# Attention's outputs normalized after the product with the values and transposed back

## The chip, the cores and the metric

The kernel runs on one core of a Trainium2 chip. Its time is the device time of one execution in microseconds. A matmul runs on TensorE (PE in the rows; PEld is its weight load), elementwise work on VectorE (DVE), ScalarE (ACT) and GpSimd (POOL); DMAs are issued mostly from SyncE's queue (SP). TensorE and the others exchange data through eight PSUM banks of 512 f32 columns on 128 partitions; GpSimd reaches SBUF only.

## The reference

Four batches, eight heads, 512 local and 32 global tokens, head size 64. A local query sees the 32 global keys and the local keys within 32 positions; a global query sees all 544. Two feed-forward nets follow. Cut to what matters:

```python
def sm(s):                                   # softmax over the last axis
    s = s - np.max(s, axis=-1, keepdims=True)
    e = np.exp(s)
    return e / (np.sum(e, axis=-1, keepdims=True) + 1e-09)
k_all, v_all = np.concatenate([k_g, k_l], axis=2), np.concatenate([v_g, v_l], axis=2)
out_g = np.matmul(sm(scale * np.matmul(q_g, k_all.transpose(0, 1, 3, 2))), v_all)
s_ll = np.where(np.abs(pos[:, None] - pos[None, :]) <= 32, scale * (q_l @ k_l^T), -1e9)
s_l = np.concatenate([scale * (q_l @ k_g^T), s_ll], axis=-1)
out_l = np.matmul(sm(s_l), np.concatenate([v_g, v_l], axis=2))
x = concatenate([out_g, out_l], axis=2), heads side by side   # 2176 tokens x 512
h = x @ moe_w_in;   x = (h * np.cos(h)) @ moe_w_out            # 512 -> 2048 -> 512
h = np.maximum(x @ moe2_w_in, 0.0);   out = (h * h) @ moe2_w_out
```

The factors on the inputs make the scores wide, so that the maximum in `sm` matters.

## The kernel before

*Attention.* The work is cut into 16 pairs p of heads (batch p // 4) and 8 global units g (two pairs each). Queries of a pair are cut into 8 tiles of 64, each against its window of 128 local keys and the 32 global ones. For a pair, TensorE transposes keys and queries (`tr_k`, `tr_q`, tiles tk, tq); `s_mm` makes 16 score blocks (s). VectorE's `top` scales, masks and finds the row maximum (line 372), eight per pair; ScalarE's `exp` (line 385) makes exponentials and row sums. `recip` (lines 396, 400) turns the sums into factors, and `norm` (line 415 on VectorE, 420 on GpSimd) and `norm_g` (line 404) multiply the probabilities pt by them. TensorE transposes the result (`tr_w`, `tr_g`, tiles tw and tg), and `g_mm` and `v_mm` multiply by the values: the values are the stationary operand, the probabilities stream, and the outputs o come with the 128 head coordinates on the rows, as the nets want them in xt. `o_evac` copies them there. The global unit does the same with 64 queries of two pairs at once (`s_mm`, `exp`, `norm` at line 530, `tr_w`, `tr_l`, `o_mm` at line 557, which writes og).

*PSUM.* Banks 0 and 1 take transposes in turn, bank 2 a score block and tg, banks 3 to 5 scores, banks 6 and 7 the outputs.

*The nets.* Weights come as 64-bit numbers: `conv` loads a raw tile of 512 KB (lines 92, 97) into one of two buffers, and ScalarE, VectorE and GpSimd make f32 from it (lines 115 to 138). `w_in` and `w_out` sum and split weights, `x_prep` sums and splits inputs (lines 147, 160, 653, 665). A step of a net has seven products (ha, he, hb by bank, line 785) and output products y (line 877); 48 steps run one after the other. The high half of a step's result g can be written only once the attention's last tiles are closed.

*Order.* Every operation is an `Op` with durations by engine. `att_graph` calls the pieces of the attention in a written sequence, and that sequence is TensorE's. The other queues are filled by a planner: it walks time forward, gives each engine the ready operation with the least due time (`latest`), and lets operations that two engines can do go to either. Each engine then runs its queue strictly in that order. `beside`, `d_v2` and `d_g2` price the operations that VectorE and GpSimd share.

## Time and profile before

| | us |
|---|---|
| three runs: median (lowest, highest) | 874.5 (872.16, 874.72) |
| profiled execution, its time | 873.02 |
| its span, first to last instruction | 871.2 |
| TensorE busy | 845.6 |
| VectorE busy | 666.0 |
| GpSimd busy | 558.2 |
| ScalarE busy | 533.7 |

The span is what the trace covers; the time has 1.82 us around it. The attention fills the first 147 us of the span, and the first output product of the nets starts at 164 us. Busy time is an average over stages of different kinds, so the rows further down are taken by stretch.

### The profile page before, as it was taken

Reading aid. Unit: us, or ns where it says so; the run is one execution under the profiler, and the core shown is the slowest. Engines: PE = TensorE matmul, PEld = TensorE weight load, DVE = VectorE, ACT = ScalarE, POOL = GpSimd, SP = SyncE. Lnnn points to the kernel's source line nnn. Section 1 sums busy time; section 2 is a strip of 40 time slices with the busy share of each in tenths; the row PEclk is TensorE's granted clock in tenths of the full one; section 3 lists DMA queues with packets and bytes.
Section 4 is the critical chain, followed back from the end, with each engine's and each line's share of the span. In section 5 each row is a group of like instructions: output and inputs, shape, how many; then the busy total and the mean of one; then the engine's idle time right before and its main releaser. Section 6 shows DMA issues by size and latency. Waiting matters only on the chain.

```text
span 871.2 us, 17208 instructions
## 1 busy us (share of the span) xinstructions
PE 845.6 (97%) x6028; PEld 781.6 (90%) x6028; DVE 666.0 (76%) x1541; ACT 533.7 (61%) x1279; POOL 558.2 (64%) x614
## 2 busy tenths in 40 slices
PE   8979997999999999999999999999999999999997
PEld 7758775899998999999999998889898989898886
DVE  6868989999799687868787799988766767454544
ACT  5867996878776566656665777756544554343331
POOL 4446799899877574557556799988444747332221
PEclk9998998899999999999999999999999999999999
DMA  9889864347865666675667366586774687346733
GB/s 174 184 219 202 188 180 170 134 183 255 313 240 202 221 218 236 224 236 183 233 238 258 135 217 250 185 271 237 271 233 143 241 297 225 131 163 247 215 120 83
DMA packets 134038, 182.00 MB, mean 209 GB/s; under 512 B 60736, under 2 KB 114496, under 8 KB 133952
## 3 DMA queue, kind: packets, MB, share of 16 engines
q1 hardware_dynamic: 130256, 179.73, 62.9%
q10 hardware_dynamic: 3696, 1.18, 0.6%
q8 instruction: 48, 0.79, 0.4%
q14 instruction: 38, 0.31, 0.1%
HBM read 141.03 MB, written 35.65 MB: 203 GB/s over the span
## 4 chain that ended last, share of the span: by engine, by line
PE 87%; ACT 4%; DVE 4%; POOL 2%; DMA 1%; issue 1%; SPq 0%; ACTq 0%; POOLq 0%
PE y L877 42%; PE hb L785 16%; PE he L785 11%; PE ha L785 10%; ACT pt L385 2%; PE tw L425 2%; PE s L360 1%; PE o L463 1%; PE tq L311 1%; PE tk L302 1%; PE sg L491 1%; PE spin L620 1%; POOL wf L138 1%; DMA raw<-in_moe_w_in_dram 1%; PE o L448 1%
## 5 line engine op out<-in xcount | busy, mean ns | idle before, releaser
L147 POOL TENSOR_TENSOR g<-cr,g 128x384 fp32r<-128x384 f32 (+1 forms) x192 | 202.2, 1060 | 161.9 <-ACT g L836 157.1
L888 DVE TENSOR_TENSOR xt<-y,xt 128x384 f32<-128x384 f32 (+2 forms) x287 | 170.2, 595 | 88.9 <-PE y L877 87.9
L877 PE MATMUL y<-g,wo 128*128 128x384 f32 (+1 forms) x1152 | 217.1, 326 | 0.0
L877 PE MATMUL y<-wo,g 128*128 128x512 f32 x816 | 209.5, 393 | 0.0
L877 PEld LDWEIGHTS y<-g,wo 128*128 128x128 f32 x1152 | 193.8, 188 | 0.0
L877 PEld LDWEIGHTS y<-wo,g 128*128 128x128 f32 x816 | 150.0, 188 | 24.3 <-DVE wo L147 0.2
L785 PE MATMUL hb<-xs,wi 128*128 128x384 f32 (+1 forms) x864 | 167.0, 328 | 4.4 <-ACT s L793 4.0
L785 PEld LDWEIGHTS hb<-xs,wi 128*128 128x128 f32 x864 | 147.9, 189 | 10.5 <-ACT s L793 4.5
L785 PE MATMUL he<-xs,wi 128*128 128x384 f32 (+1 forms) x576 | 111.9, 329 | 2.9 <-DVE cr L828 2.9
L785 PE MATMUL ha<-xs,wi 128*128 128x384 f32 (+1 forms) x576 | 111.7, 329 | 0.3 <-ACT ptg L513 0.3
L836 ACT ACTIVATE g<-cr 128x384 fp32r<-128x384 f32 (+1 forms) x192 | 95.5, 503 | 24.3 <-DVE cr L828 23.6
L785 PEld LDWEIGHTS he<-xs,wi 128*128 128x128 f32 x576 | 98.8, 189 | 8.1 <-DVE cr L828 4.0
L138 POOL TENSOR_TENSOR wf<-wf,cc 128x512 uint32<-128x512 uint32 x64 | 86.8, 1357 | 24.5 <-DVE wf L126 18.0
L785 PEld LDWEIGHTS ha<-xs,wi 128*128 128x128 f32 x576 | 98.3, 189 | 2.5 <-ACT ptg L513 0.5
L131 DVE SCALAR_TENSOR_TENSOR cc<-raw,cc 128x512 uint32<-128x512 uint32 x64 | 67.3, 1056 | 0.0
L822 ACT ACTIVATE cr<-cr,halfpi 128x384 f32<-128x384 f32 (+1 forms) x96 | 56.3, 592 | 8.2 <-DVE cr L817 7.3
L793 ACT ACTIVATE s<-hb 128x384 f32<-128x384 f32 (+1 forms) x48 | 22.7, 473 | 54.1 <-PE hb L785 53.1
L385 ACT ACTIVATE pt<-pt,st 128x160 f32<-128x160 f32 x128 | 53.1, 419 | 3.4 <-DVE st L372 3.4
L147 POOL TENSOR_TENSOR wi<-ws,wi 128x512 fp32r<-128x512 f32 x25 | 34.3, 1375 | 27.7 <-ACT wi L171 18.0
L126 DVE TENSOR_SCALAR wf<-wf 128x512 uint32<-128x512 uint32 x64 | 47.0, 737 | 6.5 <-ACT wf L115 4.0
L793 ACT ACTIVATE s<-he 128x384 f32<-128x384 f32 (+1 forms) x48 | 22.6, 471 | 42.9 <-PE he L785 42.8
L122 ACT ACTIVATE cc<-raw 128x512 uint32<-128x512 uint32 x64 | 42.3, 668 | 7.9 <-DMA raw<-in_moe_w_in_dram 7.2
(141 smaller groups left out, 1298.1 us busy)
## 6 DMA issues: line engine op xcount, KB each, us to landing
xs<-xs_T SPq DMA_DIRECT2D x48, 768.0 KB, 5.8
xs<-xs_B SPq DMA_DIRECT2D x36, 768.0 KB, 5.4
raw<-in_moe_w_in_dram SPq DMA_DIRECT2D x32, 512.0 KB, 5.5
raw<-in_moe_w_out_dram SPq DMA_DIRECT2D x32, 512.0 KB, 4.6
xs<-xs_T SPq DMA_DIRECT2D x24, 640.0 KB, 5.5
xs_T<-xs SPq DMA_DIRECT2D x16, 768.0 KB, 3.6
xs<-xs_B SPq DMA_DIRECT2D x18, 640.0 KB, 5.5
xs_B<-xs SPq DMA_DIRECT2D x12, 768.0 KB, 4.4
```

The lines of the kernel that those rows point to most:

```text
L122: A.activation(v, raw[q, m, c][:, :, 0].bitcast(U32), AF.Copy, scale=2.0**-29)
L126: V.tensor_scalar(u, u, 3, None, op0=ALU.logical_shift_left)
L131: V.scalar_tensor_tensor(v, t[:, :, 1].bitcast(U32), 0x80000000, v, op0=ALU.bitwise_and, op1=ALU.bitwise_or,)
L138: G.tensor_tensor(u, u, v, op=ALU.add)
L147: eng.tensor_tensor(lo, x, hi.bitcast(F32), op=ALU.subtract)
L385: nc.scalar.activation(self.pt[hb][:, u, :], self.pt[hb][:, u, :], AF.Exp, bias=self.st[hb][:, 0, u : u + 1], scale=-1.0, accum_out=self.s ...
L785: nc.tensor.matmul(out, lhsT=w[:, ws, c : c + P], rhs=xs[:, xh, kk, 0:n], start=start and k == 0, stop=k == 5, skip_group_check=True,)
L793: A.activation(self.sb[name], self.hold(bank_name), AF.Copy)
L822: A.activation(self.r[key], self.r[key], AF.Sin, bias=halfpi, scale=TWOPI)
L836: A.activation(GT[s, f][0][:, th * n : th * n + n], self.r[key], AF.Copy)
L877: nc.tensor.matmul(o, lhsT=l, rhs=r, start=k == 0, stop=k == 5)
L888: V.tensor_tensor(dst, y, dst, op=ALU.add)
```

## The change

The probabilities stay unnormalized. `tr_w` transposes the exponentials as they are, and GpSimd's `gather` copies the global columns without a factor. In `g_mm` and `v_mm` the operands change places: the transposed probabilities are stationary and the values stream, so that o has 64 queries of two tiles on the rows and the head coordinates on the columns. A query's factor is then one number per row, and `o_norm` (VectorE, two per pair) multiplies by it while it moves o from PSUM to the new tile OS. `tr_o` transposes OS back, four transposes per pair (tile to), and one `o_evac` per pair copies 128x512 into xt. `recip` works once per pair on eight sums. The global unit's `o_mm` writes [query, head coordinate] with 32-wide stationary tiles; `places` puts its factor into the column of the head's half, `o_norm` and one transpose (tog) bring it back.

PSUM banks 0, 1, 2 and 5 take transposes in turn (`TBANK`); scores lie in 3, 4, 6 and 7, beside the outputs in 6 and 7. The sequence of the attention is now a string, `ORDER`. In the planner, operations on SBUF that use the port shared by VectorE and GpSimd carry `port` and follow one another on it; their durations are lower; what is planned early is due 30 earlier and raw loads 60, where both had 20, and the lag of the first loads is 4.0 where it was 2.5; `BIAS` changes from 6 to -100.

```diff
-    ST = [lp.tile([P, 4, 4], F32, name=f"st{i}") for i in range(4)]
+    ST = [lp.tile([P, 4, 8], F32, name=f"st{i}") for i in range(4)]
...
+    OS = lp.tile([P, 2, 256], F32, name="os")
+    OG = lp.tile([P, P], F32, name="og_s")
+    odd = lp.tile([P, 2], F32, name="odd")
...
-        UNIT[hb, i, 0] = ((3, 5)[hb], i)
-        UNIT[hb, i, 1] = (4, k) if k < 3 else (2, 0)
+        for h in range(2):
+            UNIT[divmod(k, 2) + (h,)] = (3 + h, KTB * k) if k < 3 else (6 + h, 256)
+    ROUNDS = ((1, 1), (0, 0), (0, 1), (1, 0))
...
-        def recip(self, hb):
-            st = self.st[hb]
+        def recip(self):
+            st = self.st
             nc.vector.tensor_scalar(
                 st[:, 2, :], st[:, 1, :], 1e-9, None, op0=ALU.add, op1=ALU.add,
                 accum_out=st[:, 3, 0:1],
             )
             nc.vector.reciprocal(st[:, 2, :], st[:, 2, :])
-        def norm_g(self, hb):
-            nc.gpsimd.tensor_tensor(
+        def gather(self, hb):
...
+            nc.gpsimd.tensor_scalar(
                 self.pgs[:, hb].rearrange("p (i h q) -> p h i q", i=2, h=2),
                 self.pt[hb][:, :, P:KTB].rearrange("p (h i) q -> p h i q", h=2),
-                self.st[hb][:, 2, :].rearrange("p (h i) -> p h i", h=2)
-                .unsqueeze(3).to_broadcast([P, 2, 2, SG]),
-                op=ALU.mult,
+                **ONE,
...
-        def norm(self, hb, u, eng):
-            w, r = self.pt[hb][:, u, 0:P], self.st[hb][:, 2, u : u + 1]
-            if eng == "V":
-                nc.vector.tensor_scalar(
-                    w, w, r, None, op0=ALU.mult, op1=ALU.add,
-                    accum_out=self.st[hb][:, 3, u : u + 1],
-                )
-            else:
-                nc.gpsimd.tensor_scalar(w, w, r, 1.0, op0=ALU.mult, op1=ALU.mult)
...
-                    for h in range(2):
-                        d = slice(64 * h, 64 * h + 64)
+                    for half in range(2):
+                        q = slice(64 * half, 64 * half + 64)
                         nc.tensor.matmul(
-                            self.o[i][d, hb, :],
-                            lhsT=VGZ[self.b % 2][k, self.kk, d],
-                            rhs=self.tgs[k, hb, :],
+                            self.o[i][q, hb, :],
+                            lhsT=self.tgs[k, hb, q],
+                            rhs=VGZ[self.b % 2][k, self.kk, :],
...
-                for half in range(2):
-                    v = (VB if half else VA)[self.p // 2 % 2]
-                    q = slice(64 * half, 64 * half + 64)
-                    for h in range(2):
+                for h in range(2):
+                    for half in range(2):
+                        v = (VB if half else VA)[self.p // 2 % 2]
+                        q = slice(64 * half, 64 * half + 64)
                         nc.tensor.matmul(
-                            self.o[i][64 * h : 64 * h + 64, hb, q],
-                            lhsT=v[:, 2 * hb + i, 2 * (self.p % 2) + h, :],
-                            rhs=self.tws[hb][:, 2 * h + i, q],
+                            self.o[i][q, hb, 64 * h : 64 * h + 64],
+                            lhsT=self.tws[hb][:, 2 * h + i, q],
+                            rhs=v[:, 2 * hb + i, 2 * (self.p % 2) + h, :],
...
-        def o_evac(self, i, eng):
-            c0 = self.b * SL
-            dst = xt[:, self.kk, c0 : c0 + SL].rearrange("p (k i q) -> p k i q", k=2, i=2)
-            copy(eng, dst[:, :, i, :], self.o[i])
+        def o_norm(self, i):
+            nc.vector.tensor_tensor(
+                OS[:, i, :].rearrange("p (u d) -> p u d", d=D),
+                self.o[i].rearrange("p k (h d) -> p (k h) d", h=2),
+                self.st[:, 2, i::2].unsqueeze(2).to_broadcast([P, 4, D]),
+                op=ALU.mult,
+            )
+        def tr_o(self, k):
+            self.to = bank(k, "to")
+            for hb in range(2):
+                for i in range(2):
+                    c = (2 * hb + i) * P
+                    nc.tensor.transpose(
+                        self.to[:, c : c + P], OS[:, i, hb * P : hb * P + P], ident
+                    )
+        def o_evac(self, eng):
+            copy(eng, xt[:, self.kk, self.b * SL : self.b * SL + SL], self.to)
...
-        def norm(self):
-            nc.gpsimd.tensor_scalar(
-                self.pt, self.pt, self.st[:, 6:7], 1.0, op0=ALU.mult, op1=ALU.mult
+        def places(self):
+            st = self.st
+            nc.vector.tensor_scalar(
+                st[:, 8:10], odd, st[:, 6:7], None, op0=ALU.mult, op1=ALU.add,
+                accum_out=st[:, 10:11],
...
+            self.o = bank(6, "og")[:, 0:D]
             va = VA[self.gi % 2]
-            for i in range(2):
-                for c in range(5):
-                    for h in range(2):
-                        r = 128 if c < 4 else 32
-                        qs = slice((2 * i + h) * SG, (2 * i + h + 1) * SG)
-                        nc.tensor.matmul(
-                            self.o[64 * h : 64 * h + 64, i, :],
-                            lhsT=va[0:r, c, 2 * i + h, :],
-                            rhs=self.tws[:, c, qs] if c < 4 else self.tls[:, qs],
-                            start=(c == 0),
-                            stop=(c == 4),
-                            skip_group_check=True,
-                        )
-        def o_evac(self, eng):
-            c0 = NLOC + self.b * SG
-            copy(eng, xt[:, 2 * self.g : 2 * self.g + 2, c0 : c0 + SG], self.o)
+            for c in range(5):
+                r = 128 if c < 4 else 32
+                for j in range(4):
+                    qs = slice(j * SG, (j + 1) * SG)
+                    nc.tensor.matmul(
+                        self.o[qs, :],
+                        lhsT=self.tws[:, c, qs] if c < 4 else self.tls[:, qs],
+                        rhs=va[0:r, c, j, :],
+                        start=(c == 0),
+                        stop=(c == 4),
+                        skip_group_check=True,
+                    )
+        def o_norm(self):
+            nc.vector.tensor_tensor(
+                OG.rearrange("p (h d) -> p h d", h=2),
+                self.o.unsqueeze(1).to_broadcast([P, 2, D]),
+                self.st[:, 8:10].unsqueeze(2).to_broadcast([P, 2, D]),
+                op=ALU.mult,
+            )
+        def tr_o(self, k):
+            self.to = bank(k, "tog")[:, 0:P]
+            nc.tensor.transpose(self.to, OG, ident)
+        def o_evac(self, h, eng):
+            c0, d = NLOC + self.b * SG, slice(64 * h, 64 * h + 64)
+            src = self.to.rearrange("p (i h q) -> p i h q", i=2, h=2)
+            copy(eng, xt[d, 2 * self.g : 2 * self.g + 2, c0 : c0 + SG], src[d, :, h, :])
...
-    d_v2 = lambda n: 0.2 + n * 0.002
-    d_g2 = lambda n: 0.1 + n * 0.0026
+    d_v2 = lambda n: 0.14 + n * 0.00108
+    d_g2 = lambda n: 0.1 + n * 0.00235
...
-        u = Op({"G": 0.8, "A": 0.67}, lambda e: conv_u(q, m, c, e), ld, *wfree)
+        u = Op({"G": 0.66, "A": 0.67}, lambda e: conv_u(q, m, c, e), ld, *wfree)
         s = opA(0.67, lambda: conv_s(q, m, c), ld, *cfree)
-        v = opV(0.76 if beside[0] else 0.4, lambda: conv_v(q, m, c), u)
-        o = opV(1.0 if beside[0] else 0.65, lambda: conv_o(q, m, c), s, u)
+        v = opV(0.42, lambda: conv_v(q, m, c), u)
+        o = opV(0.69, lambda: conv_o(q, m, c), s, u)
+        v.port = o.port = "GV"
         raw_ring.free[j] = [o]
-        end = opG(1.4, lambda: conv_c(q, m, c), v, o)
+        end = opG(1.25, lambda: conv_c(q, m, c), v, o)
...
-    tring = Ring(2)
-    s_bank, o_bank = {k: [] for k in (2, 3, 4, 5)}, {0: [], 1: []}
-    tw_pt, pg_ring, tws_ring, tgs_ring = Ring(4), Ring(2), Ring(3), Ring(2)
+    tring, TBANK = Ring(4), (0, 1, 2, 5)
+    s_bank = {k: [] for k in (3, 4, 6, 7)}
+    tw_pt, pg_ring, tws_ring, tgs_ring, st_ring = Ring(4), Ring(2), Ring(3), Ring(2), Ring(4)
+    os_free, og_free = [], []
...
+            done = soft(lambda: None, s)
+            done.lag = 0.27 * (ROUNDS.index((hb, i)) + 1)
+            o = opE({"V": 0.245}, lambda e, a=(hb, i, h): x.top(*a), done, *slots[hb][1], *st_free)
...
+        x.norms = [opE({"V": 0.41}, lambda e, i=i: x.o_norm(i), o, x.rc, *os_free) for i in range(2)]
...
+    def back(p):
+        x = pairs[p]
+        k, needs = tbank(*x.norms)
+        o = opP("T", 0.436, lambda: x.tr_o(TBANK[k]), *needs)
+        os_free[:] = [o]
+        e = opE(on(512, "AV"), lambda e: x.o_evac(e), o)
+        tring.free[k] = [e]
+        oe[x.b, x.kk] = e
...
+    ORDER = (
+        "S:0 k:1 q:1 K:2 Qg:0 S:1 k:2 q:2 a:0 b:0 g:0 X:0 G:0 V:0 a:1 b:1 g:1 k:3 K:3 q:3 o:0 S:2 "
+        "G:1 V:1 w:0 k:4 o:1 S:3 O:0 L:2 a:2 b:2 g:2 q:4 x:0 X:1 G:2 V:2 a:3 b:3 Kg:1 g:3 k:5 K:4 "
+        "q:5 o:2 S:4 G:3 V:3 Z:2 w:1 k:6 o:3 S:5 O:1 L:3 a:4 Qg:1 b:4 g:4 q:6 x:1 X:2 G:4 V:4 a:5 "
...
-        o.latest -= 20
+        o.latest -= 30
+        if "Q" in o.on and hasattr(o, "raw"):
+            o.latest -= 30
...
+        if e in o.port:
+            o.end = port[0] = max(t, port[0]) + o.on[e]
...
-    BIAS, LOOK, drift = 6.0, 1.0, [0.0]
+    port = [0.0]
+    BIAS, LOOK, drift = -100, 1.0, [0.0]
```

**Where instructions move.** First place, TensorE's queue in the loop of the pairs, between the transposes of a global unit's probabilities (tlg, twg) and the next ones of a pair (tw, tg); s are scores, tk and tq transposes of keys and queries. Before:

```order
L541 MATMUL tlg<-ident,ptg 32x128
L537 MATMUL twg<-ident,ptg 128x128 x4
L360 MATMUL s<-kT_100,qT_107 64x160 x16
L557 MATMUL og<-tws_121,va_93 64x32 x8
L557 MATMUL og<-tls,va_93 64x32 x2
L557 MATMUL og<-tws_121,va_93 64x32 x8
L557 MATMUL og<-tls,va_93 64x32 x2
L425 MATMUL tw<-ident,pt_109 128x128 x4
L425 MATMUL tw<-ident,pt_110 128x128 x4
L430 MATMUL tg<-ident,pg_117 128x128 x2
```

Now:

```order
L553 MATMUL tlg<-ident,ptg 32x128
L549 MATMUL twg<-ident,ptg 128x128 x4
L307 MATMUL tk<-ident,kn 128x128 x4
L479 MATMUL to<-ident,os 128x128 x4
L365 MATMUL s<-kT_100,qT_107 64x160 x16
L569 MATMUL og<-va_93,tws_121 32x64 x16
L569 MATMUL og<-va_93,tls 32x64 x4
L418 MATMUL tw<-ident,pt_109 128x128 x4
L418 MATMUL tw<-ident,pt_110 128x128 x4
L423 MATMUL tg<-ident,pg_117 128x128 x2
L316 MATMUL tq<-ident,qn 128x128 x4
L588 MATMUL tog<-ident,og_s 128x128
```

Transposes of keys (tk) and of outputs (to) have come ahead of the scores, the global products og are one group of 20 instead of two of ten, and the transposes of queries and of the global outputs (tog) follow tg.

VectorE's queue at the same place, at the last top of a pair (the ISA rows: pt from scores s and a mask, and its minimum into st). Before:

```order
L280 COPY tws_120<-tw 128x512
L372 ISA pt_112,st_116<-s,mask_92 128x160
L372 ISA st_116 128x1
L280 COPY kT_101<-tk 128x7x64
L280 COPY kT_101<-tk 128x2x32
L396 TENSOR_SCALAR st_115<-st_115 128x4
L400 RECIPROCAL st_115<-st_115 128x4
```

Now, with the normalized outputs os made from o and the factors in st:

```order
L377 ISA pt_110,st_113<-s,mask_90 128x160
L377 ISA st_113 128x1
L467 TENSOR_TENSOR os<-o,st_116 128x256 x2
L126 TENSOR_SCALAR wf_1113<-wf_1113 128x512
L283 COPY kT_100<-tk 128x7x64
L283 COPY kT_100<-tk 128x2x32
```

The two os of the pair before stand behind the last top of the pair scored after it, where a recip of its own stood.

Second place, SyncE's queue, DMAs of keys and queries (kn, qn), values (va, vb, vgz) and raw weights. Before, around the first raw loads:

```order
L237 DMA va_94<-in_v_g_dram 32x4x64
L240 DMA va_94<-in_v_l_dram 96x4x64
L240 DMA va_94<-in_v_l_dram 128x4x64 x3
L240 DMA va_94<-in_v_l_dram 32x4x64
L92 DMA raw<-in_moe_w_in_dram 128x4x256 x2
L676 DMA xs_0_B_1070<-xs 128x1536
L247 DMA vb_96<-va_94 64x1024
L248 DMA vb_96<-va_94 64x1024
L230 DMA kn<-in_k_l_dram 128x4x64 x4
L230 DMA qn<-in_q_l_dram 128x4x64 x4
```

Now:

```order
L233 DMA kn<-in_k_l_dram 128x4x64 x4
L92 DMA raw<-in_moe_w_in_dram 128x4x256 x2
L240 DMA va_93<-in_v_g_dram 32x4x64
L243 DMA va_93<-in_v_l_dram 96x4x64
L243 DMA va_93<-in_v_l_dram 128x4x64 x3
L243 DMA va_93<-in_v_l_dram 32x4x64
L233 DMA qn<-in_q_l_dram 128x4x64 x4
L264 DMA qgn<-in_q_g_dram 32x8x64 x3
L259 DMA vgz_98<-in_v_g_dram 32x4x64 x4
L250 DMA vb_95<-va_93 64x1024
L251 DMA vb_95<-va_93 64x1024
L97 DMA raw<-in_moe_w_out_dram 128x1024 x2
```

The first raw loads have moved ahead of the values that follow the keys; two of w_out, which came much later, stand a few rows on.

Third place, GpSimd's queue at the end of the attention, from the last copies into pg on (xs, xr: inputs of the nets; wi, ws, wo: weights; g: results of a step). Before:

```order
L404 TENSOR_TENSOR pg_118<-pt_112,st_116 128x2x2x32
L420 TENSOR_SCALAR pt_112<-pt_112,st_116 128x128 x2
L530 TENSOR_SCALAR ptg<-ptg,stg_126 128x544
L147 TENSOR_TENSOR xs<-xr,xs 128x384 x2
L138 TENSOR_TENSOR wf_2029<-wf_2029,cc 128x512
L653 TENSOR_TENSOR xr<-xt,xr 128x384
L160 TENSOR_TENSOR ws<-wf_2029 128x256
L147 TENSOR_TENSOR wi<-wf_2029,wi 128x512
L147 TENSOR_TENSOR xs<-xr,xs 128x384
L147 TENSOR_TENSOR wi<-wf_2029,wi 128x256
L653 TENSOR_TENSOR xr<-xt 128x384 x3
L653 TENSOR_TENSOR xr<-xt,xr 128x384 x2
L147 TENSOR_TENSOR g_2756<-cr,g_2755 128x384
```

Now:

```order
L409 TENSOR_SCALAR pg_118<-pt_112 128x2x2x32
L681 TENSOR_TENSOR xr<-xt,xr 128x384
L117 TENSOR_SCALAR wf_2562<-raw 128x512
L681 TENSOR_TENSOR xr<-xt,xr 128x384
L147 TENSOR_TENSOR xs<-xr,xs 128x384 x4
L681 TENSOR_TENSOR xr<-xt 128x384
L138 TENSOR_TENSOR wf_2326<-wf_2326,cc 128x512
L681 TENSOR_TENSOR xr<-xt 128x384
L138 TENSOR_TENSOR wf_2562<-wf_2562,cc 128x512
L681 TENSOR_TENSOR xr<-xt,xr 128x384
L147 TENSOR_TENSOR wo<-wf_2326,wo 128x512
L147 TENSOR_TENSOR g_2763<-cr,g_2762 128x384 x2
```

The sums and splits of the second block's input weights (ws, wi) are no longer there; the parts of xr and xs that are left stand in front of the first g.

## Rows read from the trace of the kernel before

**Rows 1.** The page's first part: busy us, share of span, instructions.

```profile
PE 845.6 (97%) x6028; PEld 781.6 (90%) x6028; DVE 666.0 (76%) x1541; ACT 533.7 (61%) x1279; POOL 558.2 (64%) x614
```

**Rows 2.** Windows: length, busy by engine, granted clock, DMA share, GB/s.

```profile
60.00:80.00 20.00, 17.13 (x243) 14.41 (x244) 13.74 (x75) 14.92 (x57) 8.73 (x19) 0.74 0.94 235
...
140.00:160.00 20.00, 13.70 (x130) 12.08 (x129) 18.30 (x23) 10.92 (x22) 16.58 (x15) 0.74 0.44 171
160.00:200.00 40.00, 39.22 (x226) 39.22 (x227) 38.00 (x61) 32.91 (x65) 39.51 (x36) 1.00 0.55 207
...
72.98:87.71 14.73, 14.41 (x252) 11.28 (x250) 13.13 (x71) 12.07 (x48) 11.59 (x21) 1.00 0.88 191
```

**Rows 3.** Timeline of TensorE: start, length, line, [idle before, releaser].

```profile
18.63 0.67 PE L448 MATMUL o<-tgs,vgz 64*64 64x128 f32 x16
...
62.83 2.41 PE L360 MATMUL s<-kT,qT 64*64 64x160 f32 x30 [4.87 <-ACT tls L278]
...
72.98 0.67 PE L448 MATMUL o<-tgs,vgz 64*64 64x128 f32 x16
...
74.66 1.09 PE L425 MATMUL tw<-ident,pt 128*128 128x128 f32 x8
75.59 0.38 PE L430 MATMUL tg<-ident,pg 128*128 128x128 f32 x2
...
77.12 1.32 PE L360 MATMUL s<-kT,qT 64*64 64x160 f32 x32
...
80.54 1.32 PE L360 MATMUL s<-kT,qT 64*64 64x160 f32 x32
81.79 0.66 PE L557 MATMUL og<-tws,va 128*64 128x32 f32 x16
...
83.44 0.66 PE L425 MATMUL tw<-ident,pt 128*128 128x128 f32 x4
...
134.46 0.67 PE L448 MATMUL o<-tgs,vgz 64*64 64x128 f32 x16
...
140.06 0.67 PE L448 MATMUL o<-tgs,vgz 64*64 64x128 f32 x16
...
145.13 0.66 PE L557 MATMUL og<-tws,va 128*64 128x32 f32 x16 [1.62 <-DVE tws L280]
...
146.78 2.25 PE L785 MATMUL ha<-xs,wi 128*128 128x384 f32 x6
153.06 2.29 PE L785 MATMUL hb<-xs,wi 128*128 128x384 f32 x6 [4.03 <-ACT s L793]
...
162.99 1.20 PE L785 MATMUL ha<-xs,wi 128*128 128x384 f32 x6
164.03 2.24 PE L877 MATMUL y<-g,wo 128*128 128x384 f32 x12
```

**Rows 4.** The chain that ended last, two stretches: start, length, what.

```profile
55.65 5.06 DMA raw<-in_moe_w_in_dram
...
73.65 1.08 PE o L463 x32
```

**Rows 5.** Timeline of ScalarE, columns as in rows 3.

```profile
60.73 0.66 ACT L115 ACTIVATE wf<-raw 128x512 f32<-128x512 f32 x1 [5.87 <-DMA raw<-in_moe_w_in_dram]
```

**Rows 6.** Groups: line, engine, out<-in xcount | busy us, mean ns | idle before.

```profile
L415 DVE TENSOR_SCALAR_CACHE_REDUCE pt<-pt,st 128x128 f32<-128x128 f32 x65 | 19.4, 340 | 0.1
L420 POOL TENSOR_SCALAR pt<-pt,st 128x128 f32<-128x128 f32 x63 | 22.7, 372 | 5.3 <-DVE st L400 4.0 <-PE tk L302 1.2
L280 DVE COPY xt<-o 128x256 f32<-128x256 f32 x11 | 4.4, 416 | 0.0
L372 DVE CUSTOM_DVE_ANT_0 pt<-s,mask 128x160 f32<-128x160 f32 x128 | 34.9, 317 | 4.0 <-PE s L360 3.4
L372 DVE DVE_READ_ACCUMULATOR2_ANT st<- 128x1 f32 x128 | 10.5, 82 | 0.0
L147 POOL TENSOR_TENSOR g<-cr,g 128x384 fp32r<-128x384 f32 (+1 forms) x192 | 202.2, 1060 | 161.9 <-ACT g L836 157.1
```

237 lines of the change are left out of this document (119 added, 118 removed), and 7 rows, old and new, of the table ORDER.

## The prediction

> **What bounds the kernel now.** I read first the busy line of the page: TensorE 845.6 of 871.2 us, the next engine (VectorE) 666.0 [rows 1]. Over the span TensorE is the bound, so I looked for the stretches in which it is not. The windows show two: from 60 to 80 us its granted clock is 0.74 and from 140 to 160 us again, there with 13.70 us busy of 20 [rows 2]. Once the feed-forward steps run (from 160 us) it is busy 39.22 of 40 us at clock 1.00, while GpSimd has 39.51 and VectorE 38.00 [rows 2]. From the first output product, at 164.03 us, to the end lie 707.2 us, in which the change alters no matmul, so I follow one number: when that product starts.
>
> The timeline of TensorE gives the stages before it [rows 3]. g_mm of pair 0 starts at 18.63 us, that of pair 14 at 134.46: seven loops of two pairs and one global unit in 115.8 us. One loop without trouble, from pair 6's g_mm at 72.98 to pair 8's, takes 14.73 us with 14.41 busy at clock 1.00 [rows 2, 3]. The last loop has no k and q transposes; eight transposes take 75.59 - 74.66 = 0.93 us [rows 3]. Seven quiet loops would be 7 x 14.73 - 0.9 = 102.2 us, so 13.6 us are lost. The largest loss is the score matmuls' wait of 4.87 us before 62.83 [rows 3], and the clock is down behind it. The chain puts it on a DMA of raw weights issued at 55.65 that lands 5.06 us later, and ScalarE's timeline shows why it hurts: ScalarE's queue holds the conversion of these weights ahead of the exponentials and idles 5.87 us [rows 4, 5].
>
> From pair 15's g_mm (140.06) to 164.03 pass 24.0 us. In them the global products wait 1.62 us for a copy, an hb product 4.03 us, and an ha and that hb take 2.25 and 2.29 us at the low clock, where six such matmuls at 162.99 take 1.20, and the next instruction starts after 1.04 [rows 3].
>
> **The change, part by part.**
>
> *VectorE and GpSimd.* The rows L415 and L420 (65 x 340 ns and 63 x 372 ns) go [rows 6], and with them GpSimd's eight normalizations of the global rows. VectorE gets two o_norm per pair. The nearest row is the old output copy, 128x256 out of PSUM, 416 ns [rows 6]; I take 0.42, with 0.84 as the upper end should the broadcast second operand halve the rate, and 0.34 (L415) as the lower. VectorE was busy 13.13 of 14.73 us in the quiet loop, ScalarE 12.07 [rows 2]; neither gets more work, so nothing here lengthens a loop by mass. What they save counts only where a wait ends.
>
> *Transposes back.* Two groups of four per loop: 0.93 us, and one for the global unit: 0.12. They stand beside other 128x128 transposes in the new order. TensorE has no slack in the loop (14.41 of 14.73), so it all counts: +1.05. At the low clock it would be double.
>
> *Global outputs.* Twenty matmuls (two passes each) from 81.79 to 83.44 take 1.65 us, 41 ns a pass for 32 moving columns [rows 3]. The pairs' v_mm streams 64 columns through 64-wide stationary tiles in 1.08 us for 32 passes, 34 ns [rows 4]. Now 64 columns move against 32-wide stationary tiles. Upper end: nothing gained, 1.65. Lower end: four tiles at once. A transpose of 128 columns takes 0.93 / 8 = 0.116 us [rows 3], 64 columns half of it, and 40 passes at a quarter of that are 0.58. I take 1.1, nearer to v_mm: -0.55 a loop.
> The Trainium skill, TensorEngine Tiling (Array Packing), section Instruction Overhead, says that a matmul of few columns lasts as long as one of 60. By that rule 40 passes of 60 cycles at 2.4 GHz are an estimated 1.0 us, and the whole sum would be 0.7 us lower. The trace agrees that 32 columns are not cheaper than 64 (41 against 34 ns).
>
> *A new wait.* `to` of an odd pair stands ahead of the next scores, and its two o_norm stand on VectorE behind the eight tops of the pair scored before. A top is 317 + 82 ns [rows 6]: eight, behind the first scores, end some 3.7 us after these scores start, two o_norm at 4.5, signalled at about 4.7. TensorE meanwhile has scores, g_mm, v_mm, five transposes of the global unit and four of k. The old score-to-score distance, 80.54 - 77.12 = 3.42 us [rows 3], with 0.47 for k makes 3.9. So `to` waits 0.8 us, once a loop; queued behind it are all the following scores. Ends: 0 and 1.6. For even pairs 2 us of other transposes cover it. Sum per loop: 1.05 - 0.55 + 0.8 = +1.3, times seven +9.1.
>
> *The raw weights.* SP now has the first two loads ahead of the values of group 2, where they stood behind those of group 3, and the conversions follow on GpSimd at pair 4 and on ScalarE at pair 5. Behind the loads on SP stand keys, values and queries of the next groups; the second pair of loads needs the raw buffers back and can hold them up. The load of before landed in 5.06 us [rows 4]; a conversion that its queue reaches sooner waits, at worst as the old one did (5.87 us, rows 5). Of the 13.6 us I let 2 stay (ends: 0 and 6): -11.6. With the added work: pair 14's g_mm at 134.46 - 11.6 + 9.1, 2.5 us earlier.
>
> *The passage to the feed-forward.* The stretch from pair 14's g_mm to pair 15's was 5.60 us with two feed-forward products in it (2.1). Both now come after; one `to` comes in (0.47): 4.0. From there to the first output product: 24.0 - 4.03 - 1.62 - 3.0 (ha, hb and the he behind it, each about 1.0 shorter at full clock) + 2.1 (the two products) + 1.0 (the global unit's o_norm and its transposes) + 0.1 = 18.5 us. What lets the 4.03 go: the second block's input weights are converted by pair 14 on ScalarE, where the old order had them on VectorE and GpSimd after the last pair, and GpSimd has seven operations of about 1.06 us [rows 6] left for the first block's tiles. So 22.5 instead of 29.6: -7.1.
>
> Sum: -2.5 - 7.1 = -9.6. The later steps are kept at their time: GpSimd, at 39.51 of 40, is the cover that could go [rows 2], but the order leaves it no more work in the first six steps than before. The span becomes 861.6 us; the profiled execution took 873.02 for a span of 871.2, so the time is 863.4. The three runs have a median of 874.5 (872.16 to 874.72); the profiled one is inside them.
>
> **Rivals.**
> 1. *The raw loads stall again.* SP's loads move into loops in which the DMA engines are already busy for 0.88 of the time at 191 GB/s [rows 2]. If ScalarE or GpSimd again waits some 5 us with the clock falling behind it, about 6 of the 11.6 us are kept: 869. For it: ScalarE's queue is still in order, with converts at pair 6. Against: the loads stand far earlier than their converts.
> 2. *The gain is given back later.* Earlier steps meet GpSimd and VectorE that are not ready (39.51 and 38.00 of 40 us); TensorE then waits in the first steps for 5 to 6 us: 869.
> 3. *Slower.* o_norm at 0.84 us, twice per pair, behind the tops: the wait becomes 1.7 for odd pairs and about 0.8 for even ones, some 1.7 us a loop more and again in the passage; with the buffers 6 and 7 held so long that the next scores are late as well, 0.85 us per pair, 13.6 us in all: 877. It decides against the change from 0.6 us per pair on. For it: VectorE is 89% busy in the quiet loop. Against: the old output copy of that size took 416 ns.
> 4. *More than forecast.* The global products pack four wide (0.58), the new wait is hidden, the stalls go whole: -3.6 - 5.6 - 2 from the forecast, 852.
>
> **How the numbers follow.** Forecast 0.53 (its own range 857 to 868), more 0.15, stall again 0.14, given back 0.08, slower 0.10. A measurement of this kernel tells 0.3% (2.6 us) from no change; below 871.9 is faster. Rivals 1 and 2 lie there mostly, 0.06 of them within 0.3%. So faster 0.84, same 0.06, slower 0.10. The range goes from 851 (rival 4 whole) to 872, leaving out the slower case and little more.
>
> **What would show it.** Right: no wait of several us on ScalarE before an `s`, clock 1.00 from 20 to 120 us, loops of about 16 us between the g_mm of even pairs, `to` waiting about 0.8 us for `os` once a loop, 20 global matmuls in about 1.1 us, the first y at about 154.4 us, and 707 us from it to the end. Wrong: a raw DMA ending a wait of TensorE in the pair loop, `to` waiting for every pair, or a first y that comes early while the stretch behind it is longer than 707 us.

## The result and the profile after

The changed kernel takes 864.92 us (median of five runs, 863.49 to 867.76); the kernel before took 874.40 beside it (871.91 to 874.72). The ratio is 0.9907, with a 95% interval of 0.988 to 0.9933. The profiled execution has a span of 861.7 us in 863.49. The forecast was 863.4, for a span of 861.6. That execution is the fastest of the five. The number is met; several of the steps behind it are not, and their errors cancel. The profile says where.

The page's first part. VectorE is 52 us less busy than in [rows 1], TensorE 7.6:

```profile
PE 838.0 (97%) x6100; PEld 778.2 (90%) x6100; DVE 613.8 (71%) x1379; ACT 529.8 (61%) x1264; POOL 566.7 (66%) x598
```

Windows of the changed kernel, columns as in [rows 2]: the two stretches that had the clock at 0.74, a loop without trouble, and a new low stretch.

```profile
60.00:80.00 20.00, 16.69 (x310) 13.72 (x306) 15.58 (x76) 16.38 (x61) 14.21 (x22) 1.00 0.89 205
140.00:160.00 20.00, 17.51 (x99) 16.88 (x98) 15.89 (x25) 18.57 (x38) 17.84 (x17) 1.00 0.47 180
...
81.98:96.10 14.12, 13.92 (x260) 11.67 (x259) 13.19 (x62) 13.84 (x50) 8.70 (x16) 1.00 0.98 205
240.00:260.00 20.00, 15.86 (x82) 15.54 (x82) 16.82 (x27) 14.28 (x30) 19.47 (x17) 0.91 0.79 298
```

The two stretches at 0.74 are gone. A quiet loop takes 14.12 us where the one of [rows 2] took 14.73, although it carries nine transposes more; 16.03 was forecast.

TensorE's timeline of the changed kernel, answering to [rows 3]: first and last loops, the inside of a quiet one, the waits, the first output product.

```profile
17.78 0.77 PE L441 MATMUL o<-vgz,tgs 64*64 64x128 f32 x16
...
68.49 0.24 PE L456 MATMUL o<-vb,tws 128*64 128x64 f32 x1 [2.67 <-DMA vb<-va]
...
81.98 0.67 PE L441 MATMUL o<-vgz,tgs 64*64 64x128 f32 x16
...
83.66 1.09 PE L418 MATMUL tw<-ident,pt 128*128 128x128 f32 x8
84.59 0.38 PE L423 MATMUL tg<-ident,pg 128*128 128x128 f32 x2
...
85.68 0.60 PE L479 MATMUL to<-ident,os 128*128 128x128 f32 x4
86.21 1.32 PE L365 MATMUL s<-kT,qT 64*64 64x160 f32 x32
...
91.94 0.65 PE L569 MATMUL og<-va,tws 128*32 128x64 f32 x32
...
92.77 1.09 PE L418 MATMUL tw<-ident,pt 128*128 128x128 f32 x8
...
124.93 0.67 PE L441 MATMUL o<-vgz,tgs 64*64 64x128 f32 x16
...
128.76 0.67 PE L441 MATMUL o<-vgz,tgs 64*64 64x128 f32 x16
...
143.10 1.34 PE L814 MATMUL ha<-xs,wi 128*128 128x384 f32 x6 [2.27 <-DVE cr L857]
...
147.88 0.51 PE L906 MATMUL y<-g,wo 128*128 128x384 f32 x2
```

Six groups of transposes (two of tw, tg, tk, tq, `to`) follow each other from 83.66 to 86.21, and none has a wait in brackets. The global products last from 91.94 to 92.77, 0.83 us. The first output product starts at 147.88, 16.15 us earlier than before; forecast were 9.6. From it to the end pass 861.7 - 147.88 = 713.8 us, 6.6 more than the 707.2 that the sum kept.

What is late there: the list of TensorE's waits (engine, line, releaser: us in total, times, longest) and the chain around the first of them.

```profile
PE hb L814 <- ACT hb L825: 4.1, 1, 4.1
PE o L456 <- DMA vb<-va: 3.1, 2, 2.7
PE y L906 <- DVE wo L147: 2.7, 2, 2.3
```

```profile
239.54 5.80 DMA raw<-in_moe_w_out_dram
...
245.37 0.68 ACT cc L122
...
254.45 0.39 ACT hb L825
...
254.89 2.15 PE hb L814 x6
...
258.80 1.05 PE hb L814 x6
```

VectorE's timeline in between:

```profile
248.04 1.70 DVE L131 SCALAR_TENSOR_TENSOR cc<-raw,cc 128x512 uint32<-128x512 uint32 x1
249.66 0.96 DVE L126 TENSOR_SCALAR wf<-wf 128x512 uint32<-128x512 uint32 x1
250.54 1.48 DVE L131 SCALAR_TENSOR_TENSOR cc<-raw,cc 128x512 uint32<-128x512 uint32 x1
251.95 1.48 DVE L126 TENSOR_SCALAR wf<-wf 128x512 uint32<-128x512 uint32 x1
```

A load of raw weights lands at 245.34, and ScalarE's and VectorE's queues hold its conversion ahead of the feed-forward's own work. Nine microseconds later TensorE has waited 4.1 us and goes on at a low clock: six matmuls take 2.15 us, 1.05 once the clock is back. The larger part of the delay is VectorE's: four conversions in a row take it from 248.04 to 253.43, and the new plan prices them at 0.69 (L131) and 0.42 us (L126) each. In [rows 4, 5] a queue stood idle for the landing load; here ScalarE idles 1.18 us for it, and the queues are late by their own work.

### The profile page after: what moved, and what is told of

It is laid out like the page before. It is cut to its first block, busy times and chain, and to the rows that moved or that the text cites. A ratio compares the mean times of both kernels' runs of the same rounds, so it can differ in the third digit from the quotient of the medians.

```text
span 861.7 us, 17103 instructions
## 1 busy us (share of the span) xinstructions
PE 838.0 (97%) x6100; PEld 778.2 (90%) x6100; DVE 613.8 (71%) x1379; ACT 529.8 (61%) x1264; POOL 566.7 (66%) x598
## 3 DMA queue, kind: packets, MB, share of 16 engines
q10 hardware_dynamic: 3696, 1.18, 0.6%
## 4 chain that ended last, share of the span: by engine, by line
PE 88%; DMA 3%; ACT 3%; DVE 3%; SPq 1%; issue 1%; POOL 1%; DVEq 0%; ACTq 0%
PE y L906 43%; PE hb L814 16%; PE he L814 10%; PE ha L814 10%; PE o L456 2%; PE s L365 2%; DMA raw<-in_moe_w_out_dram 1%; DMA vb<-va 1%; PE tw L418 1%; ACT pt L390 1%; PE o L441 1%; PE sg L500 1%; PE spin L648 1%; DVE pt L377 1%; DMA raw<-in_moe_w_in_dram 1%
## 5 line engine op out<-in xcount | busy, mean ns | idle before, releaser
L147 POOL TENSOR_TENSOR g<-cr,g 128x384 fp32r<-128x384 f32 (+1 forms) x192 | 199.4, 1047 | 140.3 <-ACT g L865 137.5
L131 DVE SCALAR_TENSOR_TENSOR cc<-raw,cc 128x512 uint32<-128x512 uint32 x64 | 63.2, 995 | 0.6 <-ACT cc L122 0.3
L828 DVE TENSOR_TENSOR he<-he,s 128x384 f32<-128x384 f32 (+1 forms) x48 | 26.0, 542 | 32.2 <-ACT s L822 32.1
```

Source lines behind the costliest of these rows:

```text
L131: V.scalar_tensor_tensor(v, t[:, :, 1].bitcast(U32), 0x80000000, v, op0=ALU.bitwise_and, op1=ALU.bitwise_or,)
L147: eng.tensor_tensor(lo, x, hi.bitcast(F32), op=ALU.subtract)
L828: V.tensor_tensor(self.hold(to), self.hold(bank_name), self.sb[name], op=ALU.add)
```

## The experiments

All times below are medians, the ratio is to the kernel before on the same chip; loops, first y and the rest come from each kernel's one profiled execution (even pairs' g_mm from pair 0 to pair 14).

| kernel | us | ratio, 95% interval | seven loops | first y | from y to end |
|---|---|---|---|---|---|
| before | 874.40 | 1 | 115.8 | 164.0 | 707.2 |
| the change | 864.92 | 0.988 to 0.9933 | 107.2 | 147.9 | 713.8 |
| two banks | 876.85 | 1.0018 to 1.0045 | 122.6 | 163.7 | 710.8 |
| globals one tile at a time | 875.88 | 1.001 to 1.0042 | 115.9 | 158.5 | 715.5 |
| o_norm twice | 868.09 | 0.9915 to 0.9942 | 110.8 | 152.6 | 713.5 |
| planner of before | 864.21 | 0.9872 to 0.9909 | 107.3 | 154.5 | 705.7 |
| before + planner | 879.98 | 1.0052 to 1.0079 | 121.0 | 161.8 | 716.4 |
| before + four banks | 878.10 | 1.0038 to 1.0074 | 115.9 | 164.3 | 710.7 |
| before + global unit | 875.47 | 1.0009 to 1.0042 | 119.0 | 166.2 | 710.4 |
| BIAS 6 behind attention | 864.92 | 0.9877 to 0.9929 | 110.3 | 151.1 | 713.4 |
| both plans | 862.04 | 0.9827 to 0.9889 | 110.0 | 154.5 | 707.5 |
| both plans, later raw loads | 869.81 | 0.9935 to 0.9965 | 108.8 | 153.4 | 714.8 |
| the same, vb earlier | 866.79 | 0.9902 to 0.9934 | 107.7 | 152.9 | 709.7 |
| both plans, vb earlier | 859.64 | 0.9821 to 0.9858 | 109.2 | 152.4 | 706.1 |

One caution on the last three columns. The change, "BIAS 6" and "both plans" have the same order on every engine through the first five loops, and these take 78.3, 81.8 and 81.5 us: there the time at which a load lands moves a single trace by 3 us. In "BIAS 6" it is qgn, for which TensorE waits 3.4 us instead of 0.8; in "both plans" it is vb, for which it waits 3.15 us instead of 2.67 in the fourth loop, with the matmuls behind it (69.5 to 75.3) at a clock of 0.53. Differences of 3 us in a single trace settle nothing by themselves.

### Two transposing banks instead of four

```diff
-    tring, TBANK = Ring(4), (0, 1, 2, 5)
+    tring, TBANK = Ring(2), (0, 1)
```

> The changed kernel with its transposes on two PSUM banks (0 and 1) instead of four; all else as in the change. Theory (the four banks are what made every group of four transposes 0.44 us instead of 0.49 to 0.53, and took the last 0.8 us out of a quiet loop): the quiet loop goes from 14.12 to about 15 us, TensorE shows waits of transposes (tk, tq, tw, to) for the copies that empty the banks, seven loops are 5 to 7 us longer, the time 869 to 873. Rival (the short groups come from the order in which transposes stand beside each other, and the banks are never waited for): loop 14.1 to 14.3, time 864 to 867.

876.85 us: slower than the kernel before, and 11.9 us above the change. The loop is worse than the theory had it, 17.15 us. Its window and its timeline:

```profile
89.84:106.99 17.15, 15.20 (x260) 11.53 (x259) 13.13 (x65) 14.04 (x49) 10.10 (x18) 1.00 0.86 235
```

```profile
91.52 1.09 PE L418 MATMUL tw<-ident,pt 128*128 128x128 f32 x8
92.96 0.41 PE L423 MATMUL tg<-ident,pg 128*128 128x128 f32 x2 [0.34 <-ACT tws L281]
...
94.99 0.63 PE L479 MATMUL to<-ident,os 128*128 128x128 f32 x4 [0.50 <-DVE stg L541]
...
102.64 1.09 PE L418 MATMUL tw<-ident,pt 128*128 128x128 f32 x8
104.68 0.41 PE L423 MATMUL tg<-ident,pg 128*128 128x128 f32 x2 [0.95 <-DVE tws L283]
```

The stretch from tw to `to` that took 85.68 - 83.66 = 2.02 us with four banks takes 94.99 - 91.52 = 3.47; the second tw's two groups and tg take 105.02 - 102.64 = 2.38 up to tq instead of 1.15. Of the 3.03 us a loop, 1.75 are idle time (17.15 - 15.20 against 14.12 - 13.92) and 1.28 longer groups. The new attention sends fifteen groups of transposes a loop through these banks (eight of k, q and the weights, twg, tlg, two of tg, two `to`, tog), where the old one sent nine and had another bank for tg and tlg. The Trainium skill, Perfetto Trace Analysis, section Matmuls, says to rotate independent groups through different PSUM banks, so that the copy out of one runs beside the next; this pair of traces agrees, at 3.03 us a loop.

### Four banks on the kernel before

```diff
-        hb, i = divmod(k, 2)
-        UNIT[hb, i, 0] = ((3, 5)[hb], i)
-        UNIT[hb, i, 1] = (4, k) if k < 3 else (2, 0)
+        for h in range(2):
+            UNIT[divmod(k, 2) + (h,)] = (3 + h, KTB * k) if k < 3 else (6 + h, 256)
...
-    tring = Ring(2)
+    tring, TBANK = Ring(4), (0, 1, 2, 5)
```

(The order of the eight tops follows the new places of the scores.)

> The kernel before with four transposing banks (0, 1, 2, 5) alone: scores three units to a bank in 3 and 4 and one unit each in 6 and 7, behind the outputs; queries stay on the columns, the normalizations, the order and the planner stay. Theory (the banks remove waits of transposes for copies; the loop before had only 14.73 - 14.41 = 0.32 us idle, so at most that and the step of 0.47 instead of 0.44 can go, 0.3 to 0.8 us a loop, and scores now wait for the output copies of the pair before, which takes it back): seven loops 112 to 117 us, time 869 to 876. Rival (the banks by themselves are worth the 3 us a loop that two banks cost the changed kernel): seven loops below 100 us, time 852 to 858.

878.10: slower than before, by 2 us more than the theory's upper end; the rival is out. Freeing two banks puts a unit of the scores into the outputs' banks. Two of TensorE's waits:

```profile
PE o L447 <- DVE st L371: 5.8, 3, 3.2
...
PE s L359 <- ACT xt L278: 4.0, 1, 4.0
```

The outputs wait for the row maxima of the next scores (st): that is the price of the shared banks. The scores' wait for the copy of the outputs (xt) is the old stall by another way: ScalarE stands 6.33 us for a raw load until 88.31, with that copy behind the load's conversion, and the scores start at 89.30. The seven loops together are as long as before (115.9 us), and of the trace's 3.8 us more, 3.5 lie behind the first y. So four banks gain nothing in the old order; which part of the new kernel lets them gain is not isolated.

### The global products on one tile at a time

```diff
-            for c in range(5):
-                r = 128 if c < 4 else 32
-                for j in range(4):
...
+            for j in range(4):
...
+                for c in range(5):
+                    r = 128 if c < 4 else 32
```

> The changed kernel with the twenty global products in another order: all five of one 32-row output tile, then the next tile, where the change goes round the four tiles. Same number, same operands. Theory (the 0.83 us of the group is four tiles worked on at once): the group takes 1.3 to 1.7 us, each of eight units 0.5 to 0.9 longer, time 868 to 872. Rival (64 columns at 21 ns a pass is what a pass costs, whatever tile it is on): group 0.8 to 0.9, time 864 to 866.

875.88, 11 us above the change: the theory's mechanism at a larger size. TensorE's timeline:

```profile
112.43 0.61 PE L569 MATMUL og<-va,tws 128*32 128x64 f32 x8
112.97 0.29 PE L569 MATMUL og<-va,tls 32*32 32x64 f32 x2
113.19 0.63 PE L569 MATMUL og<-va,tws 128*32 128x64 f32 x8
...
115.56 0.66 PE L418 MATMUL tw<-ident,pt 128*128 128x128 f32 x4
```

The same forty passes last 3.13 us, 78 ns each on average; with two tiles in turn (64 wide, 32 moving columns), in [rows 3], 41 ns; with four, 21 ns. The starts of the single passes in the traces say more. In the middle of a run of equal matmuls one tile takes a pass every 55 to 59 ns, in all three orders and in v_mm as well, and passes on different tiles start 6 to 7 ns apart. At each step between the 128-row and the 32-row operands (tws, tls) the distance is 144 to 153 ns: seven such steps here, three in the old order, one in the change. So the change gains by both, more tiles side by side and fewer such steps. Whether the tile or its PSUM rows set the 55 to 59 ns is not told apart, since the two go together.

### The global unit on the kernel before

```diff
-            for i in range(2):
-                for c in range(5):
-                    for h in range(2):
+            for c in range(5):
+                for j in range(4):
...
+        x.norm = opE({"V": 0.28}, lambda e: x.o_norm(), o, x.rc, *og_free)
...
+    def g_back(gi):
```

> The kernel before with the changed global unit alone: its queries on the rows, four 32-row output tiles in turn, scaling on leaving PSUM, one transpose back; pairs, banks and planner of before. Theory (two tiles in turn cost 41 ns a pass, four 21, one 74, so the group falls from 1.65 to 0.83 us whatever stands around it): 0.82 - 0.12 us a unit, eight units, time 867 to 870, and the 0.69 us of GpSimd's scaling per unit off the way to the unit's transposes. Rival (the global products have cover in this loop, or the transpose back waits for o_norm as long as it saves): 872 to 876.

The group does fall to 0.83 us (97.36 to 98.19 in its timeline), and the time is 875.47 (the profiled execution took 878.75, so its columns in the table are on the long side). Two of TensorE's waits took its place:

```profile
PE s L362 <- ACT tls L280: 5.8, 1, 5.8
...
PE tw L427 <- POOL pt L422: 2.7, 6, 0.8
```

The scores' stall before 62.83 in [rows 3] stays, as 5.8 us, and the transposes of the weights wait for GpSimd's normalizations, which this kernel still has. The rival's time holds.

### The planner, undone and alone

```diff
-    d_v2 = lambda n: 0.14 + n * 0.00108
+    d_v2 = lambda n: 0.2 + n * 0.002
...
-        v = opV(0.42, lambda: conv_v(q, m, c), u)
+        v = opV(0.76 if beside[0] else 0.4, lambda: conv_v(q, m, c), u)
...
-        o.latest -= 30
-        if "Q" in o.on and hasattr(o, "raw"):
-            o.latest -= 30
+        o.latest -= 20
...
-    BIAS, LOOK, drift = -100, 1.0, [0.0]
+    BIAS, LOOK, drift = 6.0, 1.0, [0.0]
```

(and so on for the other numbers and the port.)

> The changed kernel's attention, order and banks with the planner's numbers and rules of before (costs beside each other, no shared port, lag 2.5, due times 20 earlier, BIAS 6). Theory (attention's part makes the whole gain, the planner's part costs the 6.6 us that came back after the first output product): first y at 148 to 150 us, from it to the end 707 to 709 us, span 856 to 859, time 858 to 861. Rival 1 (the planner's earlier raw loads are what keeps ScalarE from stalling in the pair loop): a stall of 4 to 6 us behind a raw load returns in the pair loop, first y at 153 to 156, time 862 to 868. Rival 2 (what comes back after the first y comes from the earlier start itself, whatever the planner): first y near 148, from it to the end 712 to 715, time 863 to 866.

864.21, the change's time. Its first y is at 154.5, but the rest takes 705.7: none of the three cases as written. Rival 1 has the first y and the time, but not for its reason. The early raw loads are gone (the first is issued at 74.77, not 32.5), and still TensorE has no stall behind a raw load in the loops, while ScalarE waits 2.4 us for one once. Turned round, the new planner on the old kernel:

> The kernel before with the changed planner alone (attention, its banks and its order of before). Theory (the planner's part moves the raw loads and with them the 4.87 us stall before the scores at 62.83 us, attention's part makes the loops shorter): the stall goes, quiet loop 14.7 us, first y at 156 to 159 us instead of 164.0, from it to the end 712 to 715 us, time 870 to 875. Rival 1 (the planner makes most of the gain): first y at 150 us, time 864 to 867. Rival 2 (planner alone does nothing in the pair loop): first y at 163 to 165, time 873 to 880.

879.98, the second rival's time, but not its reason, since the planner does change the loops. The scores' stall is gone, as the theory said, but the loops are 5 us longer. GpSimd is busy 83.9 us in them instead of 75.1, and its queue stands 14.6 us behind the raw loads, with the normalizations that the old attention needs behind it. A group of GpSimd in the loops, then TensorE's first two waits:

```profile
L117 POOL TENSOR_SCALAR wf<-raw 128x512 f32<-128x512 f32 x6 | 4.0, 665 | 14.6 <-DMA raw<-in_moe_w_in_dram 7.6 <-DMA raw<-in_moe_w_out_dram 7.0
```

```profile
PE tlg L541 <- POOL ptg L530: 6.3, 2, 3.7
PE tw L425 <- POOL pt L420: 2.9, 5, 1.7
```

So the planner's part gains nothing in sum: it shortens the passage (128.76 to 147.88 is 19.1 us, 25.1 with the old planner) and lengthens what follows by 8.1.

### o_norm twice

```diff
-            nc.vector.tensor_tensor(
+            for _ in range(2):
+              nc.vector.tensor_tensor(
```

> The changed kernel with every o_norm done twice (the second writes the same values), 32 more VectorE instructions of 0.42 us, planned as before. It prices o_norm at 0.84 us, the upper end and the slower rival's case. Theory (the o_norm of an odd pair ends about 0.35 us before the transposes back start, so 0.84 us more than uses that up, once a loop; the even pairs have cover): the transposes back wait 0.5 us for os once a loop, loops 14.6 us, time 868 to 871. Rival 1 (the slower rival as forecast: the buffers 6 and 7 are held too and each pair is 0.85 us later): 877 to 880. Rival 2 (VectorE has the room, nothing waits): 864 to 866.

868.09, in the theory's range; the ratio's interval still touches the change's, so only the forecast slower case (877 to 880) is clearly out. Its TensorE waits show `to` behind os for the first time:

```profile
PE to L480 <- DVE os L468: 3.0, 9, 0.4
```

That is the theory's wait, about once a loop, and the seven loops are 3.6 us longer, 0.5 each. It is not all of it: in a quiet loop copies of tw on VectorE are late too (a wait of 0.46 us of tq at 87.87), and that loop takes 15.66 us. In the change itself there is no such row. VectorE's timeline there shows why: first and last of the eight tops, and the o_norm behind them.

```profile
72.75 0.33 DVE L377 CUSTOM_DVE_ANT_0 pt<-s,mask 128x160 f32<-128x160 f32 x1 [0.64 <-PE s L365]
73.00 0.09 DVE L377 DVE_READ_ACCUMULATOR2_ANT st<- 128x1 f32 x1
73.00 0.32 DVE L377 CUSTOM_DVE_ANT_0 pt<-s,mask 128x160 f32<-128x160 f32 x1
...
74.93 0.08 DVE L377 DVE_READ_ACCUMULATOR2_ANT st<- 128x1 f32 x1
74.94 0.76 DVE L467 TENSOR_TENSOR os<-o,st 128x256 f32<-128x256 f32 x2
```

Eight tops need 74.94 - 72.75 = 2.19 us, 0.27 each: the next starts together with the read of the accumulator. Both o_norm are done at 75.70, and `to` starts at 76.05. The prediction had added the two durations of [rows 6] (0.40 each) and so had the o_norm a microsecond too late.

### Where the gain was given back

Two kernels put the planner of before back for the time behind attention: the first only BIAS, the second the costs too.

```diff
+                if adone == len(att_pe):
+                    BIAS[0] = 6.0
```

> The changed kernel, with the planner's BIAS put back from -100 to 6 from the moment the last TensorE step of attention is placed; everything before that, and all costs, as in the change. Theory (the planner's way of giving VectorE no shared work is what makes the stretch behind the first output product 713.8 us instead of 707): first y stays at 148 us, from it to the end 707 to 709, time 858 to 861. Rival (the costs without contention do it, or the early start itself): 712 to 716, time 863 to 868.

```diff
-        o.port = "GV"
+        d = {"G": 0.1 + n * 0.0026, "V": 0.2 + n * 0.002} if beside[0] else {"G": d_g2(n), "V": d_v2(n)}
+        o.port = "" if beside[0] else "GV"
```

(and so on for the costs of the conversions.)

> As the kernel with BIAS 6 behind attention, and for all work planned behind the first block also the old costs (VectorE and GpSimd slower beside each other, no shared port). Theory (the plan with contention in its costs suits the feed-forward, the plan with a port suits attention): first y at 148 to 150 us, from it to the end 705 to 708, time 856 to 860. Rival (the passage is short only because the conversions of later weights were put off, so that they are missing afterwards whatever the plan): first y near 148 and 712 to 716 from it to the end, or first y near 154 and 706 from it, time 863 to 867 either way.

BIAS alone changes nothing, as the rival had it: 864.92, 713.4 us behind the first y. With the costs that stretch is 707.5 and the time 862.04. Those two differ only in the costs and the port of later work, and with the costs TensorE waits 1.6 us behind the first y instead of 7.0 (6.8 in the change, 1.8 before). The longest of these waits, first with BIAS alone, then with the costs:

```profile
PE y L906 <- POOL g L147: 2.8, 2, 1.6
PE he L814 <- DVE cr L857: 1.9, 1, 1.9
```

```profile
PE he L815 <- DVE cr L858: 0.7, 1, 0.7
```

So that is where the 6.6 us come from: planned as if VectorE and GpSimd slowed each other only at the port, the conversions are late. Over the change's whole trace L131 and L126 take 995 and 719 ns on average (64 each), where the new plan has 0.69 and 0.42 us and the old one 1.0 and 0.76 beside GpSimd.

But only about half of it is gained in sum. The passage, from pair 14's g_mm to the first y, takes 26.2 us with the costs (128.22 to 154.46) and 23.3 without (127.84 to 151.14): 2.9 of the 5.9 us come back there. This is the rival's second shape (first y near 154, about 706 from it), with a time 1 us below its range; the theory misses first y and time. The intervals of the ratio still touch, so the gain in time is not shown; that the waits move, the stretch shows, outside the 3 us of the caution.

### Loads on SP

In the change's fourth loop (17.09 us) o waits 2.67 us for vb (68.49 above), in its second (17.45 us) 0.38. Three kernels move loads on SP, all with both plans.

```diff
-        if "Q" in o.on and hasattr(o, "raw"):
-            o.latest -= 30
```

> The kernel of both plans (the change's in attention, that of before behind it), with the raw weights' loads due 30 us later than in the change, so that the first stands behind the values and keys of group 4 on SP, not of group 2. Theory (SP's queue has no room from 28 to 78 us; the early raw loads push the copies of the values and the loads of queries late, which is what the 17 and 20 us loops are): loops 1 to 4 together 58 to 61 us instead of 67.4, first y at 148 to 151, tail 707, time 855 to 858. Rival (what the raw loads lose early they lose late: the conversions end later and the passage grows by as much): first y at 154, time 861 to 864.

869.81. Loops 1 to 4 take 59.9 us as the theory had it, but the sixth takes 19.4 (in it o waits 3.3 us for vb) and a feed-forward product waits 5.3 us for VectorE, so neither case holds for the time.

```diff
-        q_in["vb", gi] = Op({"Q": 1.2}, lambda e: copy_v(gi), o, *vb_free.get(gi - 2, []), lag=3.0)
+        o.lag = 3.0
+        c = q_in["vb", gi] = Op({"Q": 1.2}, lambda e: copy_v(gi), o, *vb_free.get(gi - 2, []), lag=4.5)
+        c.first = True
...
+    for o in attention:
+        if hasattr(o, "first"):
+            o.latest -= 12
```

> As the kernel with later raw loads, and the shifted copies of the values (vb) due 12 us earlier, so that on SP each stands directly behind the next load. Theory (a wait of o for vb of 1.4 to 3.2 us is left in the pair loop of every kernel with this attention; it goes): 1 to 3 us less than the kernel with later raw loads alone. Rival (SP then stands still behind the copy, which waits for the values to land, and the keys come later): the same time or 1 to 2 us more.

866.79, 3.0 us less, and vb is left with 0.5 us of wait where it had 5.4. The time and the wait are the theory's, but the traces do not show the one to come from the other: the loops are only 1.1 us shorter, and 5.1 of the 5.6 us between the two spans lie behind the first y.

> The kernel of both plans with the raw weights' loads where the change has them (due 60 us earlier), and the shifted copies of the values due 12 us earlier. Theory (of the 862.0 of the kernel of both plans 3 us are the wait of o for vb in the pair loop; it goes, as it went with the later raw loads): seven loops 106 to 108 us, first y at 150 to 152, time 858 to 860. Rival (SP stands behind the copies, and a load or a conversion takes the wait's place): 861 to 865.

859.64, the theory's time, and the fastest kernel of the case: 0.9821 to 0.9858 of the kernel before, clear of the change's interval, but not of that of both plans alone. Its loops miss the theory, 109.2 instead of 106 to 108. TensorE's waits:

```profile
PE tqg L271 <- DMA qgn<-in_q_g_dram: 4.8, 1, 4.8
...
PE o L456 <- DMA vb<-va: 0.9, 1, 0.9
```

The wait for vb went from 3.7 (both plans) to 0.9, and the queries of the globals, on the same queue, now land late: 4.8 instead of 0.9. So the rival's mechanism is there as well. Against both plans the span is 3.5 us shorter, 1.1 of it before pair 0's g_mm, 0.8 in the loops and 1.4 behind the first y; that the earlier vb makes the gain is not shown.

## Why the prediction was right, and where it was not

The span came out at 861.7 for 861.6: the start 0.85 us earlier than assumed, the loops 6.2 better (107.15 for 113.3), the passage 0.45 worse (22.95 for 22.5), the rest 6.6 worse. Two pairs of errors cancel. From pair 14's g_mm to the end the kernels take the same, 736.7 us before and 736.8 now (871.2 - 134.46, 861.7 - 124.93): what the passage gains, the steps behind it give back, and the whole gain is the loops' 8.7 us and 0.85 at the start. In the loops, their own length was to add 9.1 us and saves 4.3 (seven times 14.73 - 14.12); the losses were to shrink by 11.6 and shrink by 4.4. That the sum came out to 0.1 us is luck. Point by point:

- *VectorE and GpSimd.* o_norm at 0.42: it takes 419 ns (L467, 32 times). Right. But ScalarE, which was to get no more work, is busy 13.84 of 14.12 us in the quiet loop.
- *Transposes back.* +1.05 a loop: two `to` at 0.44 and tog at 0.22 to 0.26 are 1.1. Right.
- *Global outputs.* -0.55 a loop: it is 1.65 - 0.83 = 0.82. The rows had the answer: 41 ns with two tiles in turn, half of it with four. The value was chosen near v_mm instead. The rule quoted beside it, of the Trainium skill, TensorEngine Tiling (Array Packing), section Instruction Overhead, gave 1.0 us; measured are 0.83. The rule is one of the latency of a matmul; taken as the distance from pass to pass, as the prediction took it, it does not fit passes on different tiles, which start 6 to 7 ns apart here.
- *A new wait.* +0.8 a loop: none. The failed step; the tops were added up as if nothing overlapped. TensorE's side, 3.9 us, was right (72.09 to 76.05). Doubling o_norm brings the wait, and prices the slower rival: 0.84 us each cost some 3 us in all, not 13.6.
- *Four banks.* The prediction named no term for them. They are worth 11.9 us in the changed kernel, more than the whole gain. It took before's transposes (0.93 us for eight) as given and did not ask how six more groups would find a bank. The quiet loop is 1.91 us shorter than forecast: 0.8 is the wait that did not come, 0.27 the global products, and the rest, some 0.85, are mostly transposes that the sum kept at their old times. The second pair's eight tw went from 1.52 (83.44 to 84.96, with 0.25 of wait for a normalization, L415) to 0.93 (92.77 to 93.70), each tg from 0.42 (84.96 to 85.38) to 0.22 us (93.70 to 93.92).
- *The raw weights.* -11.6, with 2 us of stalls left. Seven loops of 14.12 are 98.8, so 8.3 us are still lost: 3.3 in the second loop (one-time transposes of the globals' keys and queries, and waits of 2.0), 1.5 in the next (0.6 of it waits for qn), 3.0 in the fourth (vb, 2.67), 0.6 in the last. So this term was mis-sized: rival 1's place was right, but what waits is TensorE for vb and qgn, queued on SP among the early raw loads, not ScalarE. With the raw loads later, loops 1 to 4 of the kernel of both plans take 59.9 us instead of 67.4. The scores' stall went, but the planner's early loads are not what removes it in the new attention (planner of before); on the old one they do remove it. The new attention has no normalizations on GpSimd to be held up; that this is what removes the stall, no run isolates.
- *The passage.* 22.5: 3.83 + 19.1. Right in size, although a wait of 2.27 us (before 143.10) stands in it that no term had. But it hung on the planner's order, and the steps behind it take it back whole.
- *The later steps are kept at their time.* The failed step on the other side: 713.8 for 707.2. Rival 2 had the size (5 to 6 us) and was near the reason: VectorE not ready, because of the planned costs. It had the place wrong: in the first 60 us behind the first y TensorE is busy for 60.00, and the waits come at 254.89 (4.14 us) and 529.19 (2.30 us).

So the mechanism behind the gain is only in part the one that the sum rests on. Attention with the new layout costs 2.4 us a loop more than before on two banks and 0.6 less on four, and the four-tile global products are worth 2.0 us a loop against one tile. Neither the four banks nor the global unit nor the planner alone makes the old kernel faster. The new layout of the pairs without the rest was not run, so what normalizing after the product is worth by itself stays open.
